# Sliding-window attention over a cache: two loads of values into an idle K slot and eight small GpSimd loads are added

## The chip, the cores and the metric

The kernel runs on one NeuronCore of a Trainium2 chip. The metric is device time in microseconds (us), the median over runs. One further execution was taken with the hardware profiler; its rows are what is quoted here.

## The reference

One decoding step for 32 batches with 32 query heads that share 8 key and value heads. Only the last 512 of 2048 cached positions take part.

```python
B, Sq, D = 32, 1, 512
Hq, Hkv, Sk, Dh = 32, 8, 2048, 128
W = min(4096, max(256, Sk // 4))          # 512
q = (x @ wq).reshape(B, Sq, Hq, Dh).transpose(0, 2, 1, 3)
k = jnp.repeat(k_cache[:, :, Sk - W:, :], Hq // Hkv, axis=1)
v = jnp.repeat(v_cache[:, :, Sk - W:, :], Hq // Hkv, axis=1)
p = softmax(einsum("bhqd,bhkd->bhqk", q, k) * Dh ** -0.5)
out = einsum("bhqk,bhkd->bhqd", p, v).transpose(0, 2, 1, 3).reshape(B, Sq, Hq * Dh) @ wo
```

All inputs are bf16. The window of keys is 32 x 8 x 512 x 128 values of 2 bytes, 33.6 MB, and the window of values is as much again; wq and wo are 4.2 MB each. Every one of these bytes is used once.

## The kernel before

**Tiling.** The 32 batches go in eight groups q = 0 to 7 of four batches. A group's keys are one load `Kq` of 4096 KB: 128 partitions, each one of 32 (batch, head) pairs times one of four blocks of 128 keys, 32 KB in each partition. Its values `Vq` have the same layout and come in one to four pieces (`V_PIECES`). There are two slots for keys, `K_sb[0]` and `K_sb[1]`, and two for values, `V_sb[0]` and `V_sb[1]`; group q uses slot q % 2. Before the groups start, `V_sb[1]` holds wq, and after the last keys `K_sb[0]` holds wo.

**Stages.** The query projection comes first: x is turned by TensorE (L301), multiplied by wq (L313, 32 matmuls, which need both halves of wq), copied to `Q_row` (L434, L490) and transposed by VectorE (L437). Then each group goes through these steps, named by letters in hand-written orders for each engine (`PE_OPS`, `DVE_OPS`, `ACT_OPS`): T, VectorE transposes the keys in two halves (`turn`, L445); S, TensorE multiplies them with the queries in `QBD` (L331), a layout that GpSimd prepares for each group (L289); M, X, N, the maximum, the exponential and the normalisation; E, G, B, the probabilities are brought to the layout of the value rows; P, TensorE multiplies them with the values (`pv`, L361, 32 steps for a group); C, F, D, the result is picked, folded and kept in `o_sel`. At the end L393 multiplies `o_sel` with wo, and one store writes the output.

**Loads.** The x loads are issued by ScalarE (L187). All the others are issued by the SyncE program (SP), in the order of the list `LOADS` below, after the two halves of wq (`load_wq`, 2048 KB each). All go through one hardware queue, which the profile names q1. SP runs strictly in order: where a load has to wait for a slot, all loads behind it in the list wait too. `Kq` (q >= 2) waits for the second transpose of group q - 2, `V1` for the query projection (its slot holds wq), `Vq` (q >= 2) for the last value step of group q - 2. The wo loads W0 to W2 wait for the second transpose of group 6. Consumers wait on one semaphore for each slot or piece (`sem_k`, `sem_v`, `sem_wo`).

```python
LOADS = """
K0 K1 V0.0 K2 V1.0 K3 V2.0 K4 V3.0 K5 K6 V4.0 K7 V5.0 V5.1 V6.0 V6.1 V7.0 V7.1 V7.2 V7.3 W0 W1 W2
""".split()
V_PIECES = [1, 1, 1, 1, 1, 2, 2, 4]
```

**GpSimd.** Its program prepares constants (`E_sb`, `QBD` zeros, masks; L258 to L278), waits for the transposed queries (`dve_QT`, L281), and then copies the queries of each group into `QBD` (L289), four copies a group. It issues no loads.

Of the kernel before, what the change touches and what calls it, by code (L numbers as in the profile page):

```python
# [43 lines left out]
def ops_of(text):  # L44
    return [(w[0],) + tuple(int(n) for n in w[1:].split(".")) for w in text.split()]


def bass_standalone__sliding_block_cached__sampling_kernel(
# [7 lines left out]
):  # L56
    B, Sq, D = x.shape
    _, HKV, SK, DH = k_cache.shape
    HD = wq.shape[1]
    HQ = HD // DH  # L60
    REP = HQ // HKV
    W = min(4096, max(256, SK // 4))
# [57 lines left out]
    with ExitStack() as es:  # L120
        sb = lambda name, shape, dt: es.enter_context(nc.sbuf_tensor(name, shape, dt))
        sem = lambda name: es.enter_context(nc.semaphore(name))

        K_sb = [sb(f"K_sb{i}", [P, R * DH], BF16) for i in range(2)]
        V_sb = [sb(f"V_sb{i}", [P, R * DH], BF16) for i in range(2)]
# [42 lines left out]
        sem_v = [[sem(f"sem_v{i}_{j}") for j in range(max(V_PIECES))] for i in range(2)]  # L168
        sem_wo = [sem(f"sem_wo{i}") for i in range(len(WOP))]
        sem_out = sem("sem_out")  # L170
        names = (
            "pe_xT pe_q pe_Y dve_xT dve_q dve_QT dve_m dve_r dve_y dve_c act_q act_y act_warm "
            "pool_x pool_e pool_ei pool_q pool_f pool_m pool_j pool_qbd pool_fz"
# [17 lines left out]
        def load_wq(i):  # L191

            nc.sync.dma_start(
                wq_sb[:, 2 * i:2 * i + 2, :].rearrange("p k n -> p (k n)"),
                wq.rearrange("(p k) n -> p k n", k=DKT)[:, 2 * i:2 * i + 2].rearrange("p k n -> p (k n)"),
            ).then_inc(sem_wq[i], 16)
# [4 lines left out]
        def rows(cache, q, r0=0, r1=R):  # L201
            return cache[4 * q:4 * q + 4, :, SK - W:, :].rearrange(
                "b h (k r) d -> (b h) k (r d)", k=KB)[:, :, r0 * DH:r1 * DH]

        class Waits:
# [5 lines left out]
            def __call__(self, sems):  # L211
                for end in sems:
                    key, n = end[:2], end[2]
                    if self.seen.get(key, 0) < n:
                        self.seen[key] = n
                        self.eng.wait_ge(op_sem[key], n)

        @block.sync
        def _(sp):
            wait = Waits(sp)  # L220
            load_wq(1)
            wo_r = wo.rearrange("(p i) n -> p i n", i=NI)
            for op in ops_of(" ".join(LOADS)):
                kind, q = op[0], op[1]
                if kind == "K":
                    if q >= 2:
                        wait([ends["T", q - 2, 1]])
                    sp.dma_start(K_sb[q % 2][:, :], rows(k_cache, q)).then_inc(sem_k[q % 2], 16)
                elif kind == "V":
                    if q == 1:  # L230
                        sp.wait_ge(s["pe_q"], 8)
                    if q >= 2:
                        wait([ends["P", q - 2, 31]])
                    n = R // V_PIECES[q]
                    r0 = op[2] * n
                    sp.dma_start(  # L236
                        V_sb[q % 2][:, r0 * DH:(r0 + n) * DH], rows(v_cache, q, r0, r0 + n)
                    ).then_inc(sem_v[q % 2][op[2]], 16)
                else:
                    wait([ends["T", NQ - 2, 1]])  # L240
                    i0, i1 = WOP[q]
                    sp.dma_start(  # L242
                        wo_sb[:, i0:i1, :].rearrange("p i n -> p (i n)"),
                        wo_r[:, i0:i1, :].rearrange("p i n -> p (i n)"),
                    ).then_inc(sem_wo[q], 16)
            sp.wait_ge(s["dve_y"], 2)
            sp.wait_ge(s["act_y"], 2)
            sp.dma_start(
                out.rearrange("b s n -> b (s n)"), out_sb[:, :, :].rearrange("b c n -> b (c n)")
            ).then_inc(sem_out, 16)  # L250
            sp.wait_ge(sem_out, 16)

        @block.gpsimd
        def _(pool):
            wait = Waits(pool)

            def diag(t, pattern, name):
                pool.memset(t, 0.0).then_inc(s[name], 1)  # L258
                pool.wait_ge(s[name], 1)
                pool.affine_select(  # L260
                    out=t, in_=t, compare_op=ALU.not_equal, fill=1.0,
                    base=0, pattern=pattern, channel_multiplier=1,
                ).then_inc(s[name], 1)

            diag(xsel[:, :, :], [[-1, 4], [-4, 32]], "pool_x")
            pool.memset(junk[:, :], 0.0).then_inc(s["pool_j"], 1)
            pool.memset(QBD[:, :, :, :], 0.0).then_inc(s["pool_q"], 1)
            diag(F_id[:, :, :], [[-32, 4], [-1, HQ]], "pool_f")
            diag(m_id[:, :, :, :], [[-32, 4], [-4, HKV], [-1, KB]], "pool_m")
            pool.memset(F_sb[:, :, :, :], 0.0).then_inc(s["pool_fz"], 1)  # L270

            diag(E_id[:, :, :].rearrange("p e (b h) -> p e b h", b=4),
                 [[-1, REP], [-4, 4], [-16, HKV]], "pool_ei")
            pool.memset(E_sb[:, :, :, :, :], 0.0).then_inc(s["pool_e"], 1)
            pool.wait_ge(s["pool_e"], 1)
            pool.wait_ge(s["pool_ei"], 2)
            for k in range(KB):
                pool.tensor_copy(E_sb[:, k, :, :, k], E_id[:, :, :]).then_inc(s["pool_e"], 1)  # L278
            pool.wait_ge(s["pool_e"], 5)
            pool.wait_ge(s["pool_q"], 1)  # L280
            pool.wait_ge(s["dve_QT"], 1)  # L281
            for q in range(NQ):
                if q >= 2:
                    wait([ends["S", q - 2, 1]])
                for b in range(4):
                    pr = slice(32 * b, 32 * b + 32)
                    if q or b:
                        pool.wait_ge(s["pool_qbd"], 4 * q + b)
                    pool.tensor_copy(  # L289
                        QBD[pr, q % 2].rearrange("p (w t) (h c) -> p w t h c", w=2, h=HKV)[  # L290
                            :, :, :, :, 4 * b:4 * b + 4],
                        QT_sb[pr, q].rearrange("p w (h e) t -> p w t h e", h=HKV),
                    ).then_inc(s["pool_qbd"], 1)
# [265 lines left out]
```

## Time and profile before

| What | Value |
|---|---|
| median of the runs | 187.59 us (187.53 to 187.65, 2 runs) |
| the profiled execution: time | 186.74 us |
| the profiled execution: span of its instructions | 185.0 us |
| read from HBM | 75.53 MB |
| VectorE (DVE) busy | 106.5 us (58%) |
| TensorE (PE) busy | 119.9 us (65%) |
| ScalarE (ACT) busy | 49.7 us (27%) |
| GpSimd (POOL) busy | 16.9 us (9%) |

Times in the profile are in us from the start of the span. A row of the timeline gives the start, the time that a group of like instructions took, its engine, its line in the code, its operation and its tiles. "SPq" is SyncE issuing a load; the time of an issue is that of the instruction, not of the transfer. The list of loads gives, for each line of code, how many were issued, their size and the us from issue to landing.

### The profile page before, as it was taken

The page shows a single profiled execution, that of the slowest core. Times are in us where ns is not written, and L with a number is a line of the kernel's source. Part 1 is how long each engine was busy: PE and PEld are TensorE (multiplying, and loading weights), DVE is VectorE, ACT ScalarE, POOL GpSimd, SP SyncE. Part 2 cuts the span into 40 slices and gives each one's busy share as a digit, 9 for nine tenths or more (in the row PEclk, how much of TensorE's full clock was granted, in tenths as well). Part 3 has the DMA queues.
Part 4 walks back from the last instruction along what each step waited for, and adds up shares of the span by engine and source line. Part 5 has one row for each costly group of instructions (what it writes and reads, how often), then busy time and mean ns, then how long its engine had stood idle before and what let it go on. Part 6 is the DMA issues. An engine that isn't in the chain of part 4 may idle for free.

```text
span 185.0 us, 3664 instructions
## 1 busy us (share of the span) xinstructions
PE 119.9 (65%) x1636; PEld 56.3 (30%) x1636; DVE 106.5 (58%) x106; ACT 49.7 (27%) x93; POOL 16.9 (9%) x52
## 2 busy tenths in 40 slices
PE   0089104447696597649934994342799899898943
PEld 0024000013453153314421351001345446354542
DVE  0031999994549524972298328999637996320201
ACT  3000300012925037301650154001062715420301
POOL 7900040202000110001000200020000000000000
PEclk9999965556999799687995599655569999999996
DMA  6998999999999999999999999999999999999960
GB/s 213 421 500 369 432 454 454 454 390 404 450 454 443 411 386 454 454 436 425 392 436 454 432 418 411 439 446 439 418 411 411 429 425 425 411 420 431 431 287 27
DMA packets 3872, 75.80 MB, mean 410 GB/s; under 512 B 464, under 2 KB 528, under 8 KB 656
## 3 DMA queue, kind: packets, MB, share of 16 engines
q1 hardware_dynamic: 3792, 75.53, 95.9%
q8 instruction: 13, 0.21, 0.5%
q10 hardware_dynamic: 64, 0.03, 0.1%
q14 instruction: 3, 0.02, 0.0%
HBM read 75.53 MB, written 0.03 MB: 409 GB/s over the span
## 4 chain that ended last, share of the span: by engine, by line
DMA 59%; DVE 22%; PE 9%; issue 6%; SPq 2%; ACTq 1%; DVEq 0%
DMA K_sb<-in_k_cache_dram 43%; DVE KT_sb L445 17%; DMA K_sb<-in_wo_dram 12%; PE ps L313 4%; PE ps L361 4%; DMA bd<-in_x_dram 4%; DVE QT_sb L437 2%; DVE KT_sb L434 1%; SPq L236 1%; DVE C_sb L470 1%; ACTq L187 1%; SPq L242 1%; PE ps L331 1%; DVE bd L413 0%; PE ps L393 0%
## 5 line engine op out<-in xcount | busy, mean ns | idle before, releaser
L445 DVE STREAM_TRANSPOSE KT_sb<-K_sb 128x4096 f32<-128x4096 f32 x16 | 70.5, 4431 | 9.7 <-DMA K_sb<-in_k_cache_dram 9.6
L361 PE MATMUL ps<-V_sb,bd 32*128 32x512 bf16 x1024 | 64.1, 402 | 4.3 <-DMA V_sb<-in_v_cache_dram 1.7
L331 PE MATMUL ps<-KT_sb,QBD 128*32 128x512 bf16 x256 | 26.0, 544 | 39.0 <-DVE KT_sb L445 29.8
L361 PEld LDWEIGHTS ps<-V_sb,bd 32*128 32x128 bf16 x1024 | 27.4, 98 | 38.3 <-issue 14.7
L331 PEld LDWEIGHTS ps<-KT_sb,QBD 128*32 128x32 bf16 x256 | 6.7, 115 | 55.6 <-DVE KT_sb L445 36.9
L496 ACT ACTIVATE P_f<-ps,negmax 128x512 f32<-128x512 f32 x8 | 5.5, 687 | 62.3 <-DVE negmax L453 62.3
L509 ACT ACTIVATE bd<-PTc,mask 128x512 bf16<-128x512 bf16 x31 | 20.1, 711 | 0.3
L514 ACT ACTIVATE C_sb<-ps 32x512 f32<-32x512 f32 x22 | 12.9, 587 | 23.7 <-PE ps L361 23.5
L289 POOL COPY QBD<-QT_sb 32x128 bf16<-32x128 bf16 x32 | 9.2, 287 | 106.6 <-PE ps L331 89.9
L465 DVE TENSOR_SCALAR bd<-PTc,mask 128x512 bf16<-128x512 bf16 x33 | 9.3, 348 | 15.3 <-ACT PTc L503 15.3
L470 DVE COPY C_sb<-ps 32x512 f32<-32x512 f32 x10 | 6.9, 693 | 14.5 <-PE ps L361 14.4
L373 PE MATMUL ps<-C_sb,F_sb 128*128 128x128 f32 x64 | 9.7, 298 | 5.6 <-ACT C_sb L514 5.0
L373 PEld LDWEIGHTS ps<-C_sb,F_sb 128*128 128x128 f32 x64 | 8.2, 200 | 8.4 <-ACT C_sb L514 7.2
L346 PE MATMUL ps<-P_bf,E_sb 128*128 128x128 bf16 x128 | 9.8, 237 | 1.1 <-DVE P_bf L459 1.1
L451 DVE TENSOR_REDUCE maxv<-ps 128x1 f32<-128x512 f32 x8 | 5.5, 687 | 8.4 <-PE ps L331 8.4
L503 ACT ACTIVATE PTc<-ps 128x512 bf16<-128x512 f32 x8 | 4.7, 593 | 19.6 <-PE ps L346 19.6
L346 PEld LDWEIGHTS ps<-P_bf,E_sb 128*128 128x128 bf16 x128 | 8.3, 107 | 5.1 <-DVE P_bf L459 2.5
L313 PE MATMUL ps<-V_sb,bd 128*128 128x512 bf16 x32 | 9.1, 453 | 0.8 <-DVE bd L413 0.8
L301 PE MATMUL ps<-bd 32*128 32x128 bf16 x4 | 0.6, 295 | 8.9 <-DMA bd<-in_x_dram 8.9
L434 DVE CAST KT_sb<-ps 128x512 bf16<-128x512 f32 x4 | 2.5, 682 | 6.5 <-PE ps L313 6.5
L413 DVE CAST bd<-ps 128x512 bf16<-128x512 f32 x1 | 0.7, 692 | 9.5 <-PE ps L301 9.5
L490 ACT ACTIVATE KT_sb<-ps 128x512 bf16<-128x512 f32 x4 | 2.1, 603 | 14.3 <-PE ps L313 14.3
(29 smaller groups left out, 34.3 us busy)
## 6 DMA issues: line engine op xcount, KB each, us to landing
K_sb<-in_k_cache_dram SPq DMA_DIRECT2D x8, 4096.0 KB, 25.6
V_sb<-in_v_cache_dram SPq DMA_DIRECT2D x5, 4096.0 KB, 29.4
V_sb<-in_v_cache_dram SPq DMA_DIRECT2D x4, 2048.0 KB, 20.2
V_sb<-in_wq_dram SPq DMA_DIRECT2D x2, 2048.0 KB, 9.8
V_sb<-in_v_cache_dram SPq DMA_DIRECT2D x4, 1024.0 KB, 11.8
K_sb<-in_wo_dram SPq DMA_DIRECT2D x1, 2048.0 KB, 18.8
K_sb<-in_wo_dram SPq DMA_DIRECT2D x1, 1536.0 KB, 21.8
K_sb<-in_wo_dram SPq DMA_DIRECT2D x1, 512.0 KB, 22.6
```

What stands on the lines that cost most here:

```text
L289: pool.tensor_copy(QBD[pr, q % 2].rearrange("p (w t) (h c) -> p w t h c", w=2, h=HKV)[:, :, :, :, 4 * b:4 * b + 4], QT_sb[pr, q].rearrange ...
L313: ins = pe.matmul(ps[:, n], lhsT=xT_sb[:, kt, :], rhs=wq_sb[:, kt, n * 512:(n + 1) * 512], start=kt == 0, stop=kt == DKT - 1, tile_positio ...
L331: ins = pe.matmul(S_ps[32 * c:32 * c + 32, :], lhsT=QBD[:, q % 2, 2 * w + t, c0:c0 + 32], rhs=KT_sb[:, w, :, KB * h:KB * h + KB, t], start ...
L346: ins = pe.matmul(EP_ps[:, e * R:(e + 1) * R], lhsT=E_sb[:, k, e].rearrange("p m j -> p (m j)"), rhs=P_bf[:, k * R:(k + 1) * R], start=k = ...
L361: ins = pe.matmul(O_ps[:, b, :], lhsT=bd[pr, q % 2, 4 * g:4 * g + 4].rearrange("p r h e -> p (r h e)"), rhs=V_sb[q % 2][pr, 512 * g:512 * ...
L373: ins = pe.matmul(F_ps[:, 0:P], lhsT=F_sb[:, d].rearrange("p h d -> p (h d)"), rhs=C_sb[:, q % 2, :, 32 * d:32 * d + 32], start=d == 0, st ...
L445: return dve.transpose(KT_sb[:, w].bitcast(F32).rearrange("p r c t -> p r (c t)"), K_sb[q % 2][:, :].bitcast(F32).rearrange("p (r w c) -> ...
L451: dve.tensor_reduce(maxv[:, q:q + 1], S_ps, AX.X, ALU.max).then_inc(s["dve_m"], 1)
L465: ins = dve.tensor_scalar(o, i, m, None, op0=ALU.mult)
L470: ins = dve.tensor_copy(*pick_args(q, r))
L509: ins = act.activation(o, i, ACTF.Copy, scale=m)
L514: ins = act.activation(*pick_args(q, r), ACTF.Copy)
```

## The change

Three things are added; nothing is taken out.

- SP issues two loads of 2048 KB each, right after the second half of wq and ahead of `K0`. They read the last 512 value positions of batches 0 and 1, and of batches 2 and 3, in a layout of 16 (batch, head) pairs times eight blocks of 64 keys: 128 partitions with 16 KB in each. They are written to the two halves of `K_sb[1]`. Nothing reads what they bring; `K1` overwrites it.
- SP waits for both (`sem_pair` at 32) before it issues `K1`, which writes the same slot.
- GpSimd, after it has made `E_sb` and before it waits for the transposed queries, issues eight loads of 1, 1, 2, 2, 3, 4, 8 and 1 rows of wo, 4 KB in a row, into the first partitions of `V_sb[0]`. SP waits for all eight (`sem_g`) before it issues `V0`, which overwrites them.

```diff
+        sem_pair = sem("sem_pair")
+        G_ROWS = (1, 1, 2, 2, 3, 4, 8, 1)
+        sem_g = [sem(f"sem_g{i}") for i in range(len(G_ROWS))]
...
+        def pair_rows(n):
+
+            return v_cache[2 * n:2 * n + 2, :, SK - W:, :].rearrange(
+                "b h (k r) d -> (b h) k (r d)", k=8)
+
         @block.sync
         def _(sp):
             wait = Waits(sp)
             load_wq(1)
+            for n in range(2):
+                sp.dma_start(
+                    K_sb[1][:, 8192 * n:8192 * n + 8192], pair_rows(n)
+                ).then_inc(sem_pair, 16)
...
                 if kind == "K":
+                    if q == 1:
+                        sp.wait_ge(sem_pair, 32)
                     if q >= 2:
                         wait([ends["T", q - 2, 1]])
...
                 elif kind == "V":
+                    if q == 0:
+                        for sm in sem_g:
+                            sp.wait_ge(sm, 16)
...
             pool.wait_ge(s["pool_e"], 5)
             pool.wait_ge(s["pool_q"], 1)
+            for i, n in enumerate(G_ROWS):
+                pool.dma_start(
+                    V_sb[0][0:n, 2048 * i:2048 * i + 2048],
+                    wo.rearrange("(p i) n -> p (i n)", i=4)[0:n],
+                ).then_inc(sem_g[i], 16)
             pool.wait_ge(s["dve_QT"], 1)
```

## The prediction

> **What bounds the kernel now.** I read the page's slices first. Each digit is a fortieth of the span (4.6 us).
>
> ```profile
> PE   0089104447696597649934994342799899898943
> DVE  0031999994549524972298328999637996320201
> DMA  6998999999999999999999999999999999999960
> GB/s 213 421 500 369 432 454 454 454 390 404 450 454 443 411 386 454 454 436 425 392 436 454 432 418 411 439 446 439 418 411 411 429 425 425 411 420 431 431 287 27
> ```
>
> The reader is to see that only the DMA row has no hole between the first slice and the last two. The transfers hold at 390 to 454 GB/s through stretches in which TensorE and VectorE idle, and through stretches in which both are full. Next comes the table by stretches, with the DMA engines' share and rate as its last columns (shares a little over 1 are an effect of how packets are booked to a stretch).
>
> ```profile
> 0.00:5.00 5.00, 0.00 (x0) 0.00 (x0) 0.00 (x0) 1.49 (x2) 3.94 (x13) 1.00 0.65 217
> 20.00:25.00 5.00, 0.00 (x0) 0.00 (x0) 4.93 (x3) 0.15 (x1) 0.72 (x3) 0.96 0.97 419
> 70.00:80.00 10.00, 6.40 (x80) 2.97 (x68) 7.29 (x3) 4.24 (x8) 0.00 (x0) 0.83 0.97 419
> 175.00:180.00 5.00, 2.45 (x75) 1.93 (x73) 0.60 (x1) 0.94 (x3) 0.00 (x0) 1.00 0.80 329
> 180.00:185.00 5.00, 1.50 (x64) 1.05 (x64) 0.56 (x2) 0.54 (x2) 0.00 (x0) 0.66 0.09 32
> ```
>
> The idle share is 35% of the first 5 us (1.8 us), 20% of 175 to 180 (1.0 us) and 91% of the last 5 (4.6 us), 7.4 us in all. On the page the queues' shares add up to 96.5%, so the span has 6.5 us without transfers. All idle time of the DMA engines thus lies before the first bytes and after the last: in the middle there is none that an added transfer could fill.
>
> The chain of waits agrees. Its columns are start, us, what.
>
> ```profile
> 42.27 30.61 DMA K_sb<-in_k_cache_dram
> ...
> 81.71 30.07 DMA K_sb<-in_k_cache_dram
> ...
> 121.47 19.40 DMA K_sb<-in_k_cache_dram
> ...
> 159.09 22.60 DMA K_sb<-in_wo_dram
> ```
>
> Each of these is a load that lands 20 to 31 us after its issue, though its own bytes need far less: it stands behind two or three others in the queue. So an issue that comes some us later costs nothing so long as the queue holds work. The issues by SP, and the first landings from the list of loads, give that depth:
>
> ```profile
> 1.65 1.26 SPq L228 DMA_DIRECT2D K_sb<-in_k_cache_dram  x2
> 2.95 0.60 SPq L236 DMA_DIRECT2D V_sb<-in_v_cache_dram  x1
> 32.83 0.54 SPq L228 DMA_DIRECT2D K_sb<-in_k_cache_dram  x1
> ```
>
> ```profile
> K_sb<-in_k_cache_dram SPq DMA_DIRECT2D x1, 4096.0 KB, 21.2
> V_sb<-in_wq_dram SPq DMA_DIRECT2D x1, 2048.0 KB, 12.0
> ...
> K_sb<-in_k_cache_dram SPq DMA_DIRECT2D x1, 4096.0 KB, 30.3
> V_sb<-in_v_cache_dram SPq DMA_DIRECT2D x1, 4096.0 KB, 39.3
> ```
>
> Issue plus time to landing: the second half of wq at 1.2 + 12.0 = 13.2, K0 at 1.65 + 21.2 = 22.9, K1 at 2.3 + 30.3 = 32.6, V0 at 2.95 + 39.3 = 42.3. One load of 4096 KB after another takes 9.7, 9.7 and 9.7 us. Worked out the same way, the later ones land at 53.1 (K2), 63.2 (V1), 72.9, 82.6, 92.3, 102.1, 111.8, 121.4, 131.1 and 140.9: eight more steps of 9.6 to 9.8, one of 10.1 (V1) and one of 10.8 (K2). This belt of 9.7 us for each 4 MB sets the end; the last wo piece lands at 159.09 + 22.60 = 181.7 and 3.3 us of matmul, copy and store follow.
>
> **The change part by part.** *The two value loads* carry 2 x 2048 KB = 4.19 MB, as much as one K load, at the head of the same queue. The cost is one more step of the belt: 9.7 us. Bounds from rows: at the page's best sustained slices (454 GB/s, three in a row) 9.2 us; at the slowest step seen (K2) 10.8; averaged over all 75.5 MB from 1.7 to 181.7 us, 4.19 MB took 10.0. Rows of 16 KB in a partition rather than 32 KB do not change it: wq has 16 KB rows too, and its second half landed 4.8 us after the first (0.73 + 7.7 = 8.4), which is 9.6 for 4 MB. I take 9.7, as 11 of the 13 steps up to K7 are within 0.1 of that.
>
> *What is late behind them.* K0 lands at 22.9 + 9.7 = 32.6 (with the small loads 32.8). The first transpose started at 24.03, held by the query transpose (20.38 + 3.62); now it starts at 32.8, so 8.8 us later. VectorE's two transposes end 8.8 later at 41.6, and K2, which waits for them, is issued at about 41.6 instead of 32.83. At that moment K1 (lands at 42.5) and V0 (lands at 52.2) are still in the queue, so K2's late issue is covered by 10 us; before, it was 9.4. From then on each compute step waits for bytes that land 9.9 us later and for earlier steps that end at most 9.9 later, so no load is issued more than 9.9 us later against a queue that drains 9.9 later. All later covers remain as they are, and the end moves by the belt.
>
> *Issue time of the two loads* on SP: 2 x 0.6 us (the issue rows) ahead of K0. K0's bytes can't move before 22.9 anyway: cost nothing; without a queue ahead it would be 1.2 us.
>
> *The wait on sem_pair* ends when the second pair load lands, 13.2 + 9.7 = 22.9. Behind it on SP stand K1, V0 and all the rest; only the DMA queue would feel it. K0 is then in the queue and occupies the belt until 32.6, so K1, issued at 23, has 9.6 us of cover. Cost 0. Uncovered it would cost the latency of one issue: x, the only load with an almost empty queue ahead, took 6.8 us from its last issue to its landing (the chain's row 1.95, 6.84).
>
> *The eight small loads.* GpSimd is free at 9.0 (the last E_sb copies start at 7.69 and take 1.31). It next needs to act for `QBD`, whose first user waits for the first transpose, now at 37.2; its four copies took 1.4, so GpSimd has until 35.8 for eight issues, 3.3 us for each. No row shows a load issued by GpSimd. The nearest are the x loads: four issues in 1.57 us on ScalarE, 2 to 14 KB each, all landed 6.8 us after the last. Between nothing and eight of these one after the other (8 x 6.8 = 55 us) I take the x loads' way, as they overlapped: eight issues at 1 us, landed by about 9 + 8 + 7 = 24.
>
> [...]
>
> *Their bytes*: 22 rows of 4 KB, 90 KB. Spread over all engines at 419 GB/s that is 0.2 us; if they all fell on one of the 16 (26 GB/s each) it would be 3.4 us on that engine, and the belt waits for the slowest. The x loads, 64 packets, took 0.1% of the queues' time on the page, 0.2 us; that row is the nearest. I take 0.2 and keep 0 and 3.4 for the range.
>
> *The wait on sem_g* sits ahead of V0, with K2 and all later loads behind it. SP reaches it at 23.6. K1 holds the belt until 42.5, so it is free if the small loads have landed by 42.5, some 18 us after my estimate, and each us beyond that costs one.
>
> Sum: 9.7 + 0.2 = 9.9. The profiled execution of 186.74 becomes 196.6; the median of the runs is 0.85 above it, and 187.59 + 9.9 = 197.5.
>
> [...]
>
> **The rivals.**
>
> *Not slower: the second reading of the same values is cheap.* The pair loads read exactly the bytes of V0. If V0 then came from somewhere nearer than HBM, its 9.7 us step could shrink; at 3.5 us or less the total would be within 2%, at nothing 187.8. Against it: wq, K, V and wo loads all go at one rate, so the limit looks to be in the engines that move the bytes and not in the place they come from. 0.03.
>
> *Partly hidden.* If K2's long step (10.8) came from how the loads happened to line up and goes, and the pair loads run at 454 GB/s while little else runs, 9.2 + 0.2 - 1.1 = 8.3 gives 195.9. 0.10.
>
> *A starved queue.* The small loads, of 4 KB in a queue beside one with 32 KB rows, land one at a time: 9 + 55 = 64, so V0 starts 21 us after the belt runs dry, about 219; half as slow, 9 + 27 = 36, still costs nothing. 0.04.
>
> *One lopsided engine.* The small loads fall on few engines: 9.7 + 3.4 gives 200.7; a second step of K2's sort gives 198.7. Together 0.10.
>
> **How the numbers follow.** My forecast, one step of the belt, has 0.73, with 196.8 to 198.3 of its own (9.2 to 10.5 us, and the small loads' 0.2). The range goes to 195.8 for the partly hidden case and to 199.6, half way to the lopsided engine; outside are the starved queue, the cheap second reading and a part of the lopsided one. A change under 2% (3.75 us) can't be told from none here. Every case but the cheap second reading is slower by more: slower 0.96, same 0.03, faster 0.01 for what I haven't seen.
>
> **What would show it.** Right: 79.8 MB read (75.53 + 4.19 + 0.09); K1 issued near 23 and V0 right after; the first L445 transpose at 32.8, held by K0's landing instead of by L437; K2 issued near 41.6; the DMA row still without a hole; a span near 194.9 and wo landing near 191.6. Wrong: V0 issued after 42 and a hole in the DMA row near it (starved); V0 landing much less than 9.7 after K1 (cheap second reading); a last landing far later with the mean DMA share down (lopsided).

## The result and the profile after

The changed kernel takes 207.46 us (207.23 to 207.70, 2 runs) against 187.59: a ratio of 1.106, 95% interval 1.100 to 1.112, or 19.9 us more. The prediction had 9.9 us more and a range that ended at 199.6. The direction and the place were right, the size was half of what came.

The profiled execution has a span of 205.7 us against 185.0. Its slices, the same two rows as before, 5.1 us each:

```profile
DMA  6999999999999999999999999999999999999970
GB/s 239 430 307 219 219 222 312 446 459 420 408 433 471 417 408 417 459 438 408 411 452 448 411 408 441 443 440 408 427 452 430 389 433 420 414 420 433 421 319 15
...
HBM read 79.81 MB, written 0.03 MB: 388 GB/s over the span
```

The bytes are as forecast (79.81 MB) and the row of busy shares has no hole. But from the third to the seventh slice the same full share moves 219 to 312 GB/s; the slices behind them, up to the last two, have 389 to 471. The table by stretches shows it sharper (the last three columns are TensorE's clock, the DMA engines' share, GB/s):

```profile
15.00:20.00 5.00, 4.14 (x20) 1.67 (x17) 2.33 (x4) 2.06 (x4) 0.00 (x0) 1.00 0.98 208
20.00:25.00 5.00, 0.00 (x0) 0.00 (x0) 3.76 (x2) 0.00 (x0) 0.95 (x4) 0.92 1.00 212
25.00:30.00 5.00, 0.00 (x0) 0.00 (x0) 0.00 (x0) 0.00 (x0) 1.34 (x5) 0.50 0.99 211
35.00:40.00 5.00, 0.00 (x0) 0.00 (x0) 0.00 (x0) 0.00 (x0) 0.00 (x0) 0.50 1.05 452
```

All 16 engines are booked as busy, and half as many bytes arrive as in the same stretches before (419 GB/s from 20 to 25 us): a packet takes twice its time (in the trace the value loads' packets of 16 KB take 1.2 us at the median, those of wq, as large, 0.61). The chain of waits (start, us, what) and SP's waits say which transfers these are:

```profile
2.35 32.73 DMA K_sb<-in_v_cache_dram
...
35.09 18.97 DMA K_sb<-in_k_cache_dram
```

```profile
SPq L242 <- DMA K_sb<-in_v_cache_dram: 31.5, 1, 31.5
```

The second value load lands at 35.1, where 22.9 was forecast. The list of loads gives the us to landing of the ones before it:

```profile
V_sb<-in_wq_dram SPq DMA_DIRECT2D x1, 2048.0 KB, 12.3
K_sb<-in_v_cache_dram SPq DMA_DIRECT2D x1, 2048.0 KB, 22.4
```

With their issues at 1.2 and 1.66, the second half of wq lands at 13.5, the value loads at 24.1 and 35.1: 10.6 and 11.0 us for 2.1 MB each, 21.6 together, where the belt moved 4.2 MB in 9.7 before. SP's issues show what became of the loads behind (start, us):

```profile
2.98 32.66 SPq L242 DMA_DIRECT2D K_sb<-in_k_cache_dram  x2
35.95 0.53 SPq L253 DMA_DIRECT2D V_sb<-in_v_cache_dram  x1
53.24 0.54 SPq L242 DMA_DIRECT2D K_sb<-in_k_cache_dram  x1
```

K0 is issued at 2.98; K1, the second of the first row, only when the value loads are down, V0 right behind it, and K2 at 53.2 instead of 32.8.

### The profile page after: what moved, and what is told of

It is laid out like the page before. It is cut to its first block, busy times and chain, and to the rows that moved or that the text cites. A ratio compares the mean times of both kernels' runs of the same rounds, so it can differ in the third digit from the quotient of the medians.

```text
span 205.7 us, 3678 instructions
## 1 busy us (share of the span) xinstructions
PE 120.1 (58%) x1636; PEld 56.8 (28%) x1636; DVE 106.6 (52%) x106; ACT 49.9 (24%) x93; POOL 21.1 (10%) x60
## 3 DMA queue, kind: packets, MB, share of 16 engines
HBM read 79.81 MB, written 0.03 MB: 388 GB/s over the span
## 4 chain that ended last, share of the span: by engine, by line
DMA 74%; DVE 12%; issue 5%; PE 5%; SPq 2%; DVEq 0%
DMA K_sb<-in_k_cache_dram 48%; DMA K_sb<-in_v_cache_dram 16%; DVE KT_sb L467 11%; DMA K_sb<-in_wo_dram 11%; PE ps L383 4%; SPq L253 1%; DVE C_sb L492 1%; PE ps L415 1%; PE ps L353 0%; SPq L196 0%; SPq L231 0%; SPq L259 0%; DVE maxv L473 0%; DVEq L120 0%; DVE P_bf L501 0%
## 5 line engine op out<-in xcount | busy, mean ns | idle before, releaser
L383 PE MATMUL ps<-V_sb,bd 32*128 32x512 bf16 x1024 | 63.4, 398 | 3.8 <-DMA V_sb<-in_v_cache_dram 1.9
L536 ACT ACTIVATE C_sb<-ps 32x512 f32<-32x512 f32 x22 | 12.9, 588 | 24.4 <-PE ps L383 24.2
L368 PE MATMUL ps<-P_bf,E_sb 128*128 128x128 bf16 x128 | 11.0, 254 | 0.8 <-DVE P_bf L481 0.8
L368 PEld LDWEIGHTS ps<-P_bf,E_sb 128*128 128x128 bf16 x128 | 9.3, 115 | 4.9 <-DVE P_bf L481 2.8
## 6 DMA issues: line engine op xcount, KB each, us to landing
V_sb<-in_v_cache_dram SPq DMA_DIRECT2D x4, 2048.0 KB, 20.3
```

The lines of the kernel that those rows point to most:

```text
L368: ins = pe.matmul(EP_ps[:, e * R:(e + 1) * R], lhsT=E_sb[:, k, e].rearrange("p m j -> p (m j)"), rhs=P_bf[:, k * R:(k + 1) * R], start=k = ...
L383: ins = pe.matmul(O_ps[:, b, :], lhsT=bd[pr, q % 2, 4 * g:4 * g + 4].rearrange("p r h e -> p (r h e)"), rhs=V_sb[q % 2][pr, 512 * g:512 * ...
L536: ins = act.activation(*pick_args(q, r), ACTF.Copy)
```

## The experiments

Each run below is compared with the kernel before on the same chip (186.7 to 186.9 us), and differences are of medians. Nothing reads what the two value loads bring, in the changed kernel and in all of these.

**The value loads alone.** GpSimd's eight loads and SP's wait for them are taken out:

```diff
-                    if q == 0:
-                        for sm in sem_g:
-                            sp.wait_ge(sm, 16)
...
-            for i, n in enumerate(G_ROWS):
-                pool.dma_start(
```

> The two value loads and their wait alone, without the eight small loads and theirs. Theories: (1) the split of a load into 16 groups of 8 partitions makes every packet take twice as long; (2) the source's pitch of 512 KB from one (batch, head) to the next does that; (3) the eight small loads, in flight from 9 to 35 us, halve the rate of what runs beside them. 1 and 2: as with the whole change, about 207.3 us, the pair loads landing 10.6 and 11.0 us apart. 3: full rate, 187.6 + 9.7 = 197.3.

Measured: 206.47 against 186.89 us, 19.6 more, ratio 1.104 (1.101 to 1.108). So the eight small loads aren't what halves the rate; the third theory falls.

**The small loads alone.** The two value loads and the wait on `sem_pair` are taken out.

> The eight small loads and the wait for them alone, without the two value loads. Theories 1 and 2: 187.6 + 0.2 = 187.8 us, and the small loads land in less than half the time that they took beside the pair loads (last landing 35.0 there). Theory 3: the loads beside them run at half rate for as long as the small ones are in flight, some 10 us more, about 198.

Measured: 191.57 us, 4.7 more, ratio 1.024 (1.020 to 1.027). None of the theories had this number. SP's issues, its waits and two stretches show where it comes from (last columns as above):

```profile
1.65 1.25 SPq L236 DMA_DIRECT2D K_sb<-in_k_cache_dram  x2
34.13 0.54 SPq L247 DMA_DIRECT2D V_sb<-in_v_cache_dram  x1
```

```profile
SPq L240 <- DMA V_sb<-in_wo_dram: 31.0, 4, 22.6
```

```profile
20.00:25.00 5.00, 0.00 (x0) 0.00 (x0) 4.43 (x2) 0.00 (x0) 1.14 (x4) 0.90 1.02 425
30.00:35.00 5.00, 2.48 (x24) 0.45 (x16) 2.95 (x1) 0.00 (x0) 0.01 (x1) 0.50 0.38 164
```

Beside the small loads the rate is still 425 GB/s from 20 to 25 us. The cost has another form: SP stands in the wait for them until 34.1 us, V0 is issued then instead of at 2.95, and the queue has run nearly empty (share 0.38). It is the starved queue of the prediction, in a kernel where K1 is issued at 2.3 already and is nearly through by then (2.30 + 32.9 = 35.2). In the changed kernel SP leaves the value loads' wait at 35.1, when the last small load (issued at 12.9, 22.0 us to landing) is down as well, and K0 and K1 still stand in the queue: V0 goes out at 35.95 and the share stays at 1.05.

That the wait is the cause was tried nearly by itself. The small loads go to 22 different partitions of `C_sb`, which has no other use until later, instead of the first 1 to 8 of `V_sb[0]`, and ScalarE waits for them instead of SP:

```diff
-                    if q == 0:
-                        for sm in sem_g:
-                            sp.wait_ge(sm, 16)
...
-                    V_sb[0][0:n, 2048 * i:2048 * i + 2048],
+                    C_sb[sum(G_ROWS[:i]):sum(G_ROWS[:i + 1])].rearrange(
+                        "p a b d -> p (a b d)").bitcast(BF16),
...
             act.wait_ge(s["dve_c"], 3)
+            for sm in sem_g:
+                act.wait_ge(sm, 16)
```

> The small loads alone, without the value loads, but written to 22 partitions of C_sb, which is free until 50 us or later; SP no longer waits for them, ScalarE does so before the first exponential at 38 us. If the 4.7 us of the run with the small loads alone came from SP's wait ahead of V0: nothing but the bytes is left, 186.8 + 0.2 = 187.0. If they came from the loads themselves (their packets, or GpSimd's work): 191.5 again.

Measured: 187.40 against 186.94 us, 0.5 more, ratio 1.003 (1.001 to 1.005). The packets of the eight loads cost next to nothing there; 4.2 of the 4.7 us go with the wait. What the other partitions have to do with it was not tried apart.

**Another layout, then another source.** Two runs separate the value loads' grouping from their source's pitch. The first takes the same bytes as half rows of four batches in four key blocks: 32 groups of 4 partitions, the pitch of 512 KB from one group to the next kept.

```diff
-            return v_cache[2 * n:2 * n + 2, :, SK - W:, :].rearrange(
-                "b h (k r) d -> (b h) k (r d)", k=8)
+            return rows(v_cache, 0, 64 * n, 64 * n + 64)
```

> The same bytes into the same slot at the same place, with the small loads, but each of the two loads takes half of the rows of four batches in four key blocks (32 groups of 4 partitions, 16 KB rows, the pitch of 512 KB from group to group kept) instead of two batches in eight blocks (16 groups of 8). Theory 1: full rate, 187.6 + 9.9 = 197.5 us. Theories 2 and 3: as with the change, 207.3.

Measured: 197.57 us, 10.7 more, ratio 1.056 (1.052 to 1.059). Its stretches:

```profile
15.00:20.00 5.00, 5.00 (x22) 2.11 (x20) 1.22 (x3) 1.00 (x3) 0.00 (x0) 1.00 1.02 418
20.00:25.00 5.00, 0.26 (x2) 0.00 (x0) 4.88 (x4) 1.06 (x3) 0.02 (x1) 0.79 1.01 398
```

Same bytes, same slot, same place in the queue, rows of the same 16 KB: the rate is back (the value loads are down at 25.8). The second run keeps the 16 groups of 8 and reads wo, with 129 KB from group to group:

```diff
+            return wo[2032 * n:2032 * n + 2064].rearrange(
+                "(a r) n -> a (r n)", r=129)[:, 0:65536].rearrange("a (k m) -> a k m", k=8)
```

> The two loads keep their 16 groups of 8 partitions and 16 KB rows but read wo, with a pitch of 129 KB from group to group instead of 512 KB; the small loads stay. Their bytes are other bytes, and nothing reads them. Theory 1: half rate again, about 207.3 us. Theory 2: full rate, 197.5. Theory 3: 207.3.

Measured: 207.40 us, 20.5 more, ratio 1.109 (1.105 to 1.112), slow in the same stretch:

```profile
GB/s 243 424 311 207 212 217 333 415 453 441 428 415 428 457 428 412 415 433 453 425 415 426 441 453 410 412 434 447 441 409 415 418 428 428 420 414 417 434 362 35
```

The pitch of 512 KB is not the cause, the grouping is: the changed kernel has 208 to 212 GB/s with that pitch from group to group, but the run with four batches keeps the pitch and has 398 to 418, and the run on wo leaves it and has 207 to 217.

**The same bytes without the small loads.** As the run with four batches, with the small loads and their wait taken out too.

> The run with four batches in four key blocks again, now without the eight small loads and their wait. If the two value loads in this form cost one step of the belt and the small loads some 1.0 us: 9.7 over the kernel before, about 196.6 us, and 1.0 below the run with the small loads. If the small loads cost nothing here: the same 197.6.

Measured: 197.16 against 186.68 us, 10.5 more, ratio 1.055 (1.052 to 1.058). The small loads cost 0.2 there (10.7 less 10.5); beside the half-rate loads the runs above give 0.3 to 0.9 for them (19.9 and 20.5 less 19.6). The runs of the kernel before lie 1.2 us apart, so these are small amounts and no more. SP's issues in this run:

```profile
2.94 20.64 SPq L241 DMA_DIRECT2D K_sb<-in_k_cache_dram  x2
41.64 0.54 SPq L241 DMA_DIRECT2D K_sb<-in_k_cache_dram  x1
```

K1 goes out when the wait on `sem_pair` ends, at 23.0, and K2 at 41.6. These are the times that the prediction had for the changed kernel (near 23 and near 41.6).

**More groupings.** wo once more, now as rows that follow one another, 128 groups of one partition:

```diff
+            return wo[2048 * n:2048 * n + 2048].rearrange("(p r) n -> p (r n)", r=16)
```

> The two loads read wo as 128 rows of 16 KB that follow one another (128 groups of one partition) instead of 16 groups of 8 partitions at a pitch of 129 KB; tensor, row size, slot and small loads as in that run. Theory 1 (the grouping): full rate, 186.9 + 9.7 + 1.0 = 197.6 us. A theory that wo, or 16 KB rows in this place, are slow as such: about 207.4.

Measured: 197.70 us, 11.0 more, ratio 1.058 (1.055 to 1.062): full rate.

```profile
15.00:20.00 5.00, 5.00 (x22) 2.12 (x20) 1.12 (x2) 0.91 (x2) 0.00 (x0) 1.00 0.99 405
```

Nearly the same bytes of wo are read as in 16 groups, where 1 KB in 129 is left out; only the division into groups differs. So it is not the bytes read that are slow.

Eight batches in two key blocks, 64 groups of 2:

```diff
+            return v_cache[0:8, :, SK - W + 128 * n:SK - W + 128 * n + 128, :].rearrange(
+                "b h (k r) d -> (b h) k (r d)", k=2)
```

> The two loads take values of eight batches in two key blocks: 64 groups of 2 partitions, 16 KB rows, the pitch of 512 KB kept; small loads kept. They bring other bytes, and nothing reads them. Theory 1, if only a group of 8 partitions is too long: full rate, 197.6 us. If anything but groups of 4 or of 1 is slow: half rate, 207.4.

Measured: 197.40 us, 10.7 more, ratio 1.056 (1.053 to 1.059): full rate.

```profile
15.00:20.00 5.00, 4.93 (x22) 1.99 (x20) 1.54 (x3) 1.33 (x3) 0.00 (x0) 1.00 1.01 415
```

One batch in sixteen key blocks, 8 groups of 16, four loads of 1 MB:

```diff
+            return v_cache[n:n + 1, :, SK - W:, :].rearrange(
+                "b h (k r) d -> (b h) k (r d)", k=16)
...
-            for n in range(2):
+            for n in range(4):
                 sp.dma_start(
-                    K_sb[1][:, 8192 * n:8192 * n + 8192], pair_rows(n)
+                    K_sb[1][:, 4096 * n:4096 * n + 4096], pair_rows(n)
...
-                        sp.wait_ge(sem_pair, 32)
+                        sp.wait_ge(sem_pair, 64)
```

> The same bytes as four loads of 1024 KB, one batch each in sixteen key blocks: 8 groups of 16 partitions, 8 KB rows; small loads kept. Theory 1: slower still than 16 groups; at half the rate of those (105 GB/s) 40 us for the 4.19 MB, 186.9 + 40 + 1 = 228 us; if only the number of engines at work halves, each at full rate, 207.4. If the trouble were special to 16 groups: 197.6.

Measured: 229.91 us, 43.2 more, ratio 1.228 (1.223 to 1.234). Its rows of 8 KB are not the reason: the last value loads of the kernel before (V7, four of 1 MB) have them too, in 32 groups, and run at 424 GB/s from 160 to 170 us. The stretches show two things:

```profile
25.00:30.00 5.00, 0.00 (x0) 0.00 (x0) 0.00 (x0) 0.00 (x0) 2.01 (x7) 0.50 1.00 157
40.00:45.00 5.00, 0.00 (x0) 0.00 (x0) 0.00 (x0) 0.00 (x0) 0.00 (x0) 0.50 0.51 121
60.00:65.00 5.00, 0.00 (x0) 0.00 (x0) 0.00 (x0) 0.00 (x0) 0.00 (x0) 0.50 1.06 433
```

From 40 to 45 us the share is 0.51: half of the engines carry the load and the others have nothing left (the trace has mostly 8 packets under way at a time there, and 16 from 25 to 30 us). Eight engines at full rate would, by an estimate from the 419 of before, move half of it, or 210 GB/s; they move 121. From 25 to 30 all engines are busy, the other half already with K0, whose own grouping is fast, and the sum is 157 GB/s. K0's packets, the only ones of 32 KB, take 3.3 us each there, where the same packets of the kernel before take 1.2; so the load's engines slow down the others as well. The two share something beyond that load's own source rows; the trace doesn't name it.

**Half the partitions.** The last question was whether a group of 8 is slow as such, or the partitions that are written at one time. Two batches in four key blocks make 16 groups of 4, the first load in partitions 0 to 63 and the second in 64 to 127:

```diff
-                "b h (k r) d -> (b h) k (r d)", k=8)
+                "b h (k r) d -> (b h) k (r d)", k=4)
...
-                    K_sb[1][:, 8192 * n:8192 * n + 8192], pair_rows(n)
+                    K_sb[1][64 * n:64 * n + 64, :], pair_rows(n)
```

> The same bytes as two loads of two batches in four key blocks: 16 groups of 4 partitions, 32 KB rows, the first load into partitions 0 to 63 of the slot and the second into 64 to 127; small loads kept. If a group of 8 partitions is what is slow: full rate, 186.8 + 9.7 + 1 = 197.5 us. If what counts is on which partitions the 16 DMA engines write at one time, and a half of the partitions has only half of the ways in: half rate, 207.

Measured: 208.17 us, 21.2 more, ratio 1.113 (1.109 to 1.117).

```profile
20.00:25.00 5.00, 0.00 (x0) 0.00 (x0) 3.69 (x2) 0.00 (x0) 1.02 (x4) 0.89 0.98 205
```

Groups of 4 at half rate: groups of 8 are not needed for it. But this run also keeps 16 groups at the source, so it can't tell whether the number of groups counts or the set of partitions that is written at one time. By the rates, 16 groups ran at 205 to 217 GB/s, 32, 64 and 128 groups at 398 to 418, and 8 groups at 121 with half of the engines at work. The partition order of each engine is not in the trace, and why 32 groups are fast is open. So what the grouping acts on is not shown.

**One load of the two.** `range(2)` becomes `range(1)` and the wait 16.

> Only one of the two value loads (batches 0 and 1 in eight key blocks, 2.1 MB), with its wait at 16; small loads kept. If each load in this layout costs its bytes at half rate: half of the change's cost for them, 186.8 + 10 + 0 to 1 = 197 to 198 us, as much as both loads cost at full rate. If the slowness were one toll for the layout, not by bytes: 4.9 + 10 = 15 over the kernel before, about 202.

Measured: 197.46 us, 10.5 more, ratio 1.055 (1.052 to 1.058): half of the whole change's cost. The price goes by the bytes in this layout: 2.1 MB cost as much as 4.2 MB in any of the three fast layouts. The run also shows the wait for the small loads by itself, as the value load is down at 23.5 and SP stands before V0 until the last small load lands at 35.2:

```profile
35.32 0.54 SPq L253 DMA_DIRECT2D V_sb<-in_v_cache_dram  x1
```

K1 lands at 44.9 (23.50 + 21.4) and V0 at 54.6 (35.32 + 19.3), 9.7 later: the wait is covered and costs nothing.

## Why the prediction was wrong

**What bounds the kernel: right.** The queue's belt sets the end; nearly every added us of transfer came out at the end (21.6 us for the loads instead of 9.7, K0 21.5 us later than before, and the span 20.7 longer). One reading was loose: the row of rates has 369, 386 and 500 GB/s beside the 390 to 454 that I gave.

**The step that failed** is the first term of the sum: "The cost is one more step of the belt: 9.7 us", with "Rows of 16 KB in a partition rather than 32 KB do not change it". The second is true (16 KB rows ran at 398 to 418 GB/s in 32, 64 and 128 groups), but I compared sizes of rows where the grouping was what differed. All loads of keys, values and weights in the kernel before have 32 groups of 4 or 128 of 1; none of its rows could speak for 16 groups of 8, and I set bounds from them all the same. The term measured 19.6 us (the value loads alone), where a fast grouping costs 10.5. The landing of the last wo piece, 181.7 us in the kernel before, shows it without what comes after. The chain of the run with the value loads alone has it so:

```profile
178.93 22.50 DMA K_sb<-in_wo_dram
```

It lands at 201.4 there, 19.7 us later than before. In the run with four batches and no small loads it is issued at 169.07 and takes 22.4 to landing, which is 191.5, 9.8 us later. The step of 9.7 was thus right for the groupings that it was taken from, and the grouping is some 10 us by the landings (9.1 by the times, 19.6 less 10.5), nearly the whole of the miss. The other 0.7 of the 10.5 come behind the last load, partly perhaps from the spread of the runs; they are not explained.

**What is late behind them: the mechanism right, the sizes doubled.** K0 landed at 44.4 (32.8 forecast), the first transpose began at 44.44, held by K0's landing as forecast; K2 went out at 53.24 (41.6). With a fast grouping and no small loads the forecast times come out to 0.2 us, as shown above. The chain has no new wait of an engine for another:

```profile
44.44 8.77 DVE L467 STREAM_TRANSPOSE KT_sb<-K_sb 128x4096 f32<-128x4096 f32 x2 [20.64 <-DMA K_sb<-in_k_cache_dram]
```

**The wait on sem_pair: free, as forecast.** K1 goes out at 35.1, K0 lands at 44.4 and K1 at 54.1, 9.7 later, so the queue never lacked it.

**The small loads: the size about right, the landing 11 us later than forecast.** GpSimd issued the eight in 4.11 us, half of what I took. The last landed at 34.9 and not at 24:

```profile
9.33 4.11 POOL L299 DMA_DIRECT2D V_sb<-in_wo_dram  x8 [0.30 <-POOL E_sb L295]
```

The last of them, of 4 KB, took 22.0 us from issue to landing; in the run with four batches, beside the same rows at full rate, 12.1:

```profile
V_sb<-in_wo_dram POOLq DMA_DIRECT2D x1, 4.0 KB, 22.0
```

```profile
V_sb<-in_wo_dram POOLq DMA_DIRECT2D x1, 4.0 KB, 12.1
```

The value loads kept SP until 35.1, so the wait for the small ones never came last here. It would have been free without that too, as forecast: in the run with one value load SP stood in it until 35.2, with K1 in the queue, and V0 still landed 9.7 us after K1. The rival "a starved queue" is a real mechanism, worth 4.2 us where K1 goes out at 2.3, and decided nothing here.

**The other rivals.** V0 lands at 63.75 (35.95 + 27.8), 9.7 after K1, so a second reading of the same values is no cheaper. The partly hidden case had one thing right: K2's long step went (10.8 before; now 53.24 + 20.3 = 73.5, 9.8 after V0), which gave back 1 us. The lopsided engine is not ruled out in small: in the run with four batches K0 lands at 35.5 with the small loads (2.95 + 32.5) and at 32.7 without (2.94 + 29.8), though the total differs by 0.2 and the share stays near 1. The rows don't name engines. The lower end of my own range, 196.8, left out the 0.2 of the small loads; nothing hangs on it.

## What to carry to other kernels

A load's price is not its bytes alone: before an added load is priced by its neighbours' rate, compare how both spread the partitions over the source's slowest dimension. Of the layouts here 16 KB rows in 32, 64 or 128 groups cost 10.5 to 11.0 us for 4.2 MB, 16 groups some twice that (19.6 to 20.5) and 8 groups (of 8 KB rows) four times (43.2); a full DMA share beside half the GB/s (0.98 to 1.00 beside 208 to 212) is the sign. And a wait on the queue that issues all loads was free here only for as long as bytes queued ahead of it: nothing with K1 in the queue (V0 landed 9.7 us after it in the run with one value load), 4.2 us where the queue ran nearly empty (share 0.38).

## What the runs showed of the hardware that was not expected

- A load on half of the engines slows down the loads on the other half: 157 GB/s with all 16 busy (share 1.00), 121 with eight (0.51), against 419 to 433 otherwise (8 groups of 16 partitions).
- Eight small loads from GpSimd, issued 0.5 us apart, land one after another at a pace that follows the packets beside them: from first to last 17.5 to 34.9 us beside the half-rate loads (2.5 us each), 15.0 to 25.2 beside 16 KB rows at full rate (1.5), 15.6 to 34.0 beside 32 KB rows at full rate (2.6). That is about two of the packets beside them each time (1.2, 0.61 and 1.2 us). The load of 4 KB behind the seven others took 22.0, 12.1 and 21.1 us in these three runs.
- TensorE's granted clock was 0.50 through 25 to 50 us of the changed kernel, in which it was nearly idle (busy for 1.06 us), as it was from 25 to 45 us of the kernel before; nothing in the chain waited for it there.
